# One core, gated long convolution plus a two-layer feed-forward block: row scales through DRAM, six-bank runs in the second transform stage, new stage shares

## Chip, cores and metric

The kernel runs on one core of one Trainium2 chip. The metric is the device time of one execution in microseconds (us). Before the change it is 1026.62 us, the median of 3 runs (1026.29 to 1029.05).

## What is computed

The inputs are x (called q in the first function), k and v of 2048 rows by 576 columns, all in float32; the feed-forward part has 4608 hidden columns.

```python
def _A_ref(q, k, v, shift_k, ssm_k, ssm_D):
    k_shift = sum over t < 4 of k_pad[:, t:t+S, :] * shift_k[:, 3-t]      # short causal filter
    kv = k_shift * v
    kv_f, kf_f = rfft(kv padded to 2S), rfft(ssm_k padded to 2S)          # long causal filter
    y = irfft(kv_f * kf_f)[:S] + kv * ssm_D
    return q * y
def _B_ref(x, w1, w2):
    return relu(x @ w1) @ w2

xn = layernorm(x)
return x + _A_ref(xn, k, v, shift_k, ssm_k, ssm_D) + _B_ref(xn, w1, w2)
```

(The sums and transforms of the first function are written short here.)

## The kernel before

**Two streams in one program.** The feed-forward part ("FFN") is the main program. The convolution ("conv") is a Python generator, `conv()`, whose steps are put between the FFN's instructions while the program is written down. So one order per engine holds both, and an engine that waits at the head of its order keeps everything behind it waiting.

**The FFN.** The 16 row tiles t of 128 rows form 4 blocks; two halves of two blocks are worked one after the other. For each half there are 18 groups of 256 hidden columns, so 36 groups ("quads", L630) g in all. In a quad the hidden sums of two blocks are made by products in a Strassen-like form: `product` (L575, six matmuls of 512 columns, high and low parts of operands and weights) and `rest` (L584, two matmuls) write two PSUM banks `psh`, that trade roles as x and y. VectorE and ScalarE add, negate and take the relu between products: u2 (L686), the negated copy L688 (`x = -y`, which must have read bank y before the next `rest` writes there), p5 (L693), and `hidden` (L589), which writes the high part hh on ScalarE and the low part ll on VectorE (L595). Between the products stand eight "units" (`mm2`, L726): 12 matmuls of 288 columns into one of two double banks `pso` (tags o0, o1), then an addition to the accumulator on VectorE (L752). A unit is opened (its bank pair taken) one unit ahead, L635. Weights come by GpSimd's queue (`load_w1`, `load_w2`), ScalarE and GpSimd split them into high and low parts (L514, L515). The first three groups are done plainly (`classical`, L598); from then on the operands are multiplied by each row's 1/std.

**Row scales before.** `inv_std` (L190) gives rstd, one value per row, with rows on partitions. The operands have rows along the free axis, so the scale must be spread over all partitions: eight VectorE instructions build diagonal matrices (`diagonal`, L315), two float32 matmuls with a matrix of ones sum them (`scales`, L323, L327), two ScalarE copies leave PSUM (L330), and `scaled` multiplies (L340).

**The conv's stages**, in order: (FB) rows of the second half are normalised and transposed on VectorE (`later_operands`, L403); (FS) 14 steps combine and split operands and store them (L461 to L476), and from n = 6 on every second step loads one of 16 blocks of the long filter (`load_filter`, L807, on GpSimd's queue); the other blocks follow with a pause KT_GAP each (L865); (FK) 32 filter copies and 11 groups of first-stage transforms, with matrices loaded by GpSimd's queue (`load_mat`, L817); (FX) the short filter ("taps", L937 to L949, eight VectorE instructions per tile t) and 9 groups of input transforms; (FM) the second stage: 18 chunks n, each with the filter's spectrum, the product with the input's spectrum, a join, and the way back; (FO) 16 tiles of inverse first-stage transforms, gate and addition.

**FM before.** A step takes PE for a "run" of matmuls in 64x64 tiles: `product_of(n)` fills two `psf` banks and, in a borrowed `pso` pair, the spectrum n + 1 (16 matmul records); VectorE multiplies (L1051, four instructions), ScalarE copies the spectrum out (L1024, two), SP's queue swaps halves by eight DMAs (L1029, L1056). `join(n)` (L1063) at the start of the next step adds what the L1056 transfers brought. After every second chunk a run of its own, `way_back` (L1065), takes two chunks back: two narrow banks and a borrowed pair.

**Order and pace.** `tick` (L1180) is called with each FFN piece's columns. It advances the conv's clock by `rate` times the columns and takes up to two steps of the generator while that clock is not negative; a step costs its W_ constant. A run that borrows a bank pair is put only after a product or a rest and only if a unit has closed since the last borrowing. A negative yield is a pause in FFN columns. The constants are L57 to L63, the rate is L1173, so a stage's share of the FFN's columns is its number of steps by its W_ over `CONV_TOTAL`.

```python
rate = CONV_TOTAL / (SHARE * FFN_TOTAL - PAUSES * PAUSE - 12 * KT_GAP)
```

Of the kernel before, what the change touches and what calls it, by code (L numbers as in the profile page):

```python
# [99 lines left out]
def h3_ffn_kernel(ctx: ExitStack, tc, x, k, v, shift_k, ssm_k, ssm_D, w1, w2, fwd, inv, mid, out):  # L100
# [29 lines left out]
    hl_n = dram.tile([HB, P, 512], F32, name="hl_n")  # L130

# [183 lines left out]
    def diagonal(pool, b):  # L315
        diag = pool.tile([P, 2, D], F32, tag="xn", name=f"diag{b}", bufs=4)
        diag = diag[:, 0, :BT * P].rearrange("p (i n) -> p i n", i=BT)
        for i in range(BT):
            nc.vector.tensor_scalar(diag[:, i, :], ident, rstd[:, b * BT + i:b * BT + i + 1],
                                    None, op0=OP.mult)  # L320
        return diag

    def scales(pool, b, diag):  # L323

        ps = fft_psum()
        with tc.issue_after(done["pe"].ins):
            done["pe"] = nc.tensor.matmul(ps, ones, diag.rearrange("p i n -> p (i n)"),  # L327
                                          start=True, stop=True)
        row[b] = pool.tile([P, 512], F32, tag=f"row{b}", name=f"row{b}")
        nc.scalar.activation(row[b], ps, AF.Copy)  # L330
# [72 lines left out]
    def later_operands(view, views, load_filter):  # L403
# [8 lines left out]
        for t0 in range(first, T, 4):  # L412
            for t in range(t0, t0 + 4):
                with here():
                    stats(t, rows[t - t % 2][:, t % 2, :])
                yield W_FB / 2
            with here():
                inv_std(t0, 4)
            yield W_FB / 2
# [169 lines left out]
    def hidden(g, b, f, ps):  # L589
# [3 lines left out]
        done["act"] = nc.scalar.activation(hh, ps, AF.Relu)  # L593
        with tc.issue_after(done["centred"].ins):
            nc.vector.scalar_tensor_tensor(ll, ps, 0.0, hh, op0=OP.max, op1=OP.subtract)  # L595
        hid[g, b, f] = (hh, ll)

# [32 lines left out]
    def quad(g, units):  # L630


        def unit(n):
            if n + 1 < len(units):
                open_unit(*units[n + 1], n + 1 in stage["seeded"] and more)  # L635
            mm2(*units[n])
            post(1)
# [9 lines left out]
        open_unit(*units[0])  # L647
# [41 lines left out]
        hidden(g, 0, 1, u2)  # L689
# [4 lines left out]
        hidden(g, 1, 1, p5)  # L694
# [11 lines left out]
        hidden(g, 1, 0, x)  # L706

# [5 lines left out]
    stage = {"seeded": ()}  # L713
    seeded = set()

# [10 lines left out]
    def mm2(g, b, i):  # L726
# [5 lines left out]
        cols = slice(i * P, (i + 1) * P)  # L732
        ps, slot["closed"] = open_ps.pop((g, t))
# [67 lines left out]
    def stages(view, views):  # L801
# [5 lines left out]
        def load_filter():  # L807
            if blocks:
                d, h = blocks.pop(0)
                src = ssm_k[h * NH + d:h * NH + d + KD, :].rearrange("d (p t) -> p d t", t=A2)  # L810
                with here():
                    nc.gpsimd.dma_start(kt[halves(h)[0], d:d + KD, :], src)  # L812
# [4 lines left out]
        def load_mat(key, t):  # L817
            nc.gpsimd.dma_start(mats.put(key), fwd[t])
# [49 lines left out]
        for t in range(2):  # L868
            load_mat(("k", t), t)
# [47 lines left out]
        for e, t2 in enumerate(order):  # L917
# [13 lines left out]
            if e % U and e // U + 2 < T:  # L931
                load_mat(("k", e // U + 2), e // U + 2)
# [109 lines left out]
        def product_of(n):  # L1042
# [4 lines left out]
            leave = second_spectrum(n + 1) if n + 1 in pairs_n else lambda: None  # L1047
# [9 lines left out]
            leave()  # L1057
            load(zx, n + 2, "x")
# [6 lines left out]
        def way_back(n):  # L1065


            narrow, wide = [fft_psum() for _ in range(2)], borrowed()
            for i, banks in enumerate((narrow, [wide[:, k, :] for k in range(2)])):
                turn(banks, [(1, parts[0][n + i])])  # L1070
            for k in range(2):
                with here():
                    nc.scalar.activation(backs[:, k, :], narrow[k], AF.Copy)
            nc.sync.dma_start(both(zy, n), backs[:, :2])
            with here():
                nc.scalar.activation(backs[:, 2:], wide, AF.Copy)
            nc.sync.dma_start(both(zy, n + 1), backs[:, 2:])
# [8 lines left out]
        for n in range(NCH // 2 + 1):  # L1086
            if n in pairs_n:
                yield "wide"
            if n:
                join(n - 1)  # L1090
            if n in pairs_n:
                product_of(n)
            yield W_FMK / 2 + W_FMX
            if n and n % 2 == 0:
                yield "wide"
                way_back(n - 2)
            if n:
                yield W_FMK / 2 + W_FMB
# [74 lines left out]
    rate = CONV_TOTAL / (SHARE * FFN_TOTAL - PAUSES * PAUSE - 12 * KT_GAP)  # L1173
# [40 lines left out]
    ones = const.tile([P, P], F32, name="ones")  # L1214
    nc.vector.memset(ones, 1.0)
# [11 lines left out]
    with tc.tile_pool(name="fa", bufs=1) as fa:  # L1227
# [19 lines left out]
        diag = {b: diagonal(fa, b) for b in (1, 0)}  # L1247

        def unit(g, b, i, upto):
            open_unit(g, b, i)  # L1250
# [33 lines left out]
    for b in range(2):  # L1284
        for i in range(BT):
            open_unit(QUADS - 1, b, i)
            mm2(QUADS - 1, b, i)
# [28 lines left out]
```

## Time and profile before

The profile is of one execution. Its own span is 1026.2 us; the three timed runs took 1029.05, 1026.29 and 1026.62 us, so the span and the time of such an execution lie within half a microsecond of each other.

| Engine | busy, us | share of the span |
|---|---|---|
| PE (matmul) | 1011.8 | 99% |
| PEld (weight load) | 845.9 | 82% |
| VectorE (DVE) | 709.2 | 69% |
| GpSimd (POOL) | 486.8 | 47% |
| ScalarE (ACT) | 429.7 | 42% |

The stages lie in the span about so: FB 124 to 173 us, FS 175 to 237, filter blocks to 245, FK 285 to 379, taps 394 to 657, FM 667 to 914, FO 929 to 1005. A timeline row gives start, length, engine, line, what is written from what, how many instructions are merged, and in brackets the idle time before it with what ended it. In a table by windows each engine has its busy time in that stretch and, in parentheses, its instructions; PEclk is the granted clock as a share of full speed.

### The profile page before, as it was taken

How to read it: one execution, taken by the hardware profiler on the slowest of the kernel's cores; microseconds unless marked ns; L12 is line 12 of the kernel's file. 1: busy time of each engine (PE TensorE's matmuls, PEld its weight loads, DVE VectorE, ACT ScalarE, POOL GpSimd, SP SyncE). 2: the span in 40 equal slices, each digit the busy share in tenths (PEclk: the TensorE clock that was granted, in tenths of full speed). 3: DMA queues.
4: the chain of work that ended last, by engine and by line, in shares of the span. 5: the costliest groups of instructions: out<-in, count | busy, mean ns of one | idle time of the engine just before them, and what ended most of it. 6: DMA issues, size and time to landing. Idle time of an engine off the chain costs nothing.

```text
span 1026.2 us, 17380 instructions
## 1 busy us (share of the span) xinstructions
PE 1011.8 (99%) x6506; PEld 845.9 (82%) x6506; DVE 709.2 (69%) x1075; ACT 429.7 (42%) x761; POOL 486.8 (47%) x532
## 2 busy tenths in 40 slices
PE   9999999999999999999999999989999999999997
PEld 5898999998988889888878889867767777788777
DVE  6787677776465567779787889456656676656765
ACT  7244334443344444444434444444535355332220
POOL 4335446659544557555545455414423344344450
PEclk9999999999999999999999999999999999999999
DMA  7114467558245565369943433677778887857784
GB/s 177 48 44 117 116 173 168 181 175 200 73 134 174 179 196 146 112 208 370 277 139 125 137 97 115 205 222 222 228 227 245 236 264 238 225 189 238 207 256 116
DMA packets 92249, 184.70 MB, mean 180 GB/s; under 512 B 32082, under 2 KB 44500, under 8 KB 91268
## 3 DMA queue, kind: packets, MB, share of 16 engines
q1 hardware_dynamic: 73588, 123.47, 39.8%
q0 software_dynamic: 18256, 59.22, 20.0%
q10 hardware_dynamic: 320, 0.88, 0.3%
q8 instruction: 51, 0.84, 0.3%
q14 instruction: 34, 0.28, 0.1%
HBM read 119.04 MB, written 45.61 MB: 160 GB/s over the span
## 4 chain that ended last, share of the span: by engine, by line
PE 87%; DVE 4%; POOL 2%; DMA 2%; issue 2%; ACT 1%; SPq 1%; DVEq 0%; POOLq 0%; ACTq 0%
PE pso L571 40%; PE psh L571 34%; PE psf L765 5%; PE psg L765 4%; PE psh_c L571 3%; DMA area<-area 1%; POOL area L812 1%; PE psw L1223 1%; DMA r<-in_w 1%; DVE area L944 1%; DVE area L1051 1%; DVE area L945 0%; SPq L1029 0%; DVE sums L527 0%; DVE x L295 0%
## 5 line engine op out<-in xcount | busy, mean ns | idle before, releaser
L571 PE MATMUL pso<-w,hh 128*128 128x288 f32 x2304 | 468.4, 297 | 0.0
L571 PEld LDWEIGHTS pso<-w,hh 128*128 128x128 f32 x2304 | 378.6, 188 | 34.8 <-issue 15.6
L571 PE MATMUL pso<-w,ll 128*128 128x288 f32 x1152 | 340.0, 295 | 0.0
L752 DVE TENSOR_TENSOR acc<-pso,acc 128x576 f32<-128x576 f32 x243 | 183.0, 754 | 157.4 <-PE pso L571 157.1
L571 PEld LDWEIGHTS pso<-w,ll 128*128 128x128 f32 x1152 | 216.8, 188 | 0.0
L515 POOL TENSOR_TENSOR wb<-sums,wb 128x512 fp32r<-128x512 f32 x33 | 51.2, 1552 | 236.1 <-ACT wb L514 208.5
L515 POOL TENSOR_TENSOR w<-r,w 128x576 fp32r<-128x576 f32 x72 | 107.8, 1505 | 106.9 <-ACT w L514 105.8
L571 PE MATMUL psh<-x,wa 128*128 128x512 f32 x396 | 102.9, 395 | 0.5 <-POOL wa L515 0.3
L571 PE MATMUL psh<-xs,wb 128*128 128x512 f32 x396 | 102.0, 393 | 0.0
L571 PE MATMUL psh<-hl,wr 128*128 128x512 f32 x264 | 85.9, 407 | 6.3 <-ACT psh L688 6.3
L571 PEld LDWEIGHTS psh<-x,wa 128*128 128x128 f32 x396 | 72.3, 188 | 16.1 <-POOL wa L515 0.8
L571 PEld LDWEIGHTS psh<-xs,wb 128*128 128x128 f32 x396 | 70.8, 188 | 11.4
L515 POOL TENSOR_TENSOR wa<-r,wa 128x512 fp32r<-128x512 f32 x36 | 53.7, 1490 | 52.8 <-ACT wa L514 52.8
L595 DVE SCALAR_TENSOR_TENSOR ll<-psh,hh 128x512 fp32r<-128x512 f32 x66 | 45.2, 685 | 40.9 <-ACT hh L593 40.7
L688 ACT ACTIVATE psh<-psh 128x512 f32<-128x512 f32 x33 | 19.2, 582 | 128.2 <-DVE u L686 128.2
L571 PEld LDWEIGHTS psh<-hl,wr 128*128 128x128 f32 x264 | 46.0, 188 | 27.1 <-issue 13.2
L765 PE MATMUL psf<-area 64*64 64x512 f32 (+10 forms) x592 | 61.1, 473 | 0.0
L593 ACT ACTIVATE hh<-psh 128x512 fp32r<-128x512 f32 x66 | 39.4, 597 | 49.7 <-PE psh L571 49.0
L765 PE MATMUL psg<-area 64*64 64x512 f32 (+10 forms) x568 | 55.3, 453 | 0.0
L593 ACT ACTIVATE hh<-p 128x512 fp32r<-128x512 f32 x33 | 20.9, 632 | 79.1 <-DVE p L693 43.2
L1024 ACT ACTIVATE area<-psg 128x1024 f32<-128x1024 f32 x34 | 33.2, 1025 | 48.7 <-PE psg L765 48.1
L1051 DVE TENSOR_TENSOR area<-psf,area 128x512 f32<-128x512 f32 x72 | 44.7, 681 | 9.4 <-DMA area<-area 6.7
(140 smaller groups left out, 1525.1 us busy)
## 6 DMA issues: line engine op xcount, KB each, us to landing
r<-in_w POOLq DMA_DIRECT2D x70, 288.0 KB, 3.4
area<-area SPq DMA_DIRECT2D x144, 128.0 KB, 3.8
r<-in_w POOLq DMA_DIRECT2D x35, 512.0 KB, 5.1
zk<-area SPq DMA_DIRECT2D x64, 144.0 KB, 2.3
area<-zk SPq DMA_DIRECT2D x18, 512.0 KB, 4.5
area<-zx SPq DMA_DIRECT2D x18, 512.0 KB, 3.9
zy<-area SPq DMA_DIRECT2D x18, 512.0 KB, 4.8
area<-zy SPq DMA_DIRECT2D x32, 288.0 KB, 5.4
```

Of the source, the lines that this page charges most:

```text
L515: nc.gpsimd.tensor_tensor(w[:, 1, :n], src, w[:, 0, :n], OP.subtract)
L571: last = nc.tensor.matmul(ps, a, m, start=start and n == 0, stop=n == len(seq) - 1, skip_group_check=True)
L593: done["act"] = nc.scalar.activation(hh, ps, AF.Relu)
L595: nc.vector.scalar_tensor_tensor(ll, ps, 0.0, hh, op0=OP.max, op1=OP.subtract)
L688: nc.scalar.activation(x, y, AF.Copy, scale=-1.0)
L752: done["acc"] = nc.vector.tensor_tensor(two(acc[t]), ps[:, :, :NH], two(acc[t]), OP.add)
L765: done["pe"] = nc.tensor.matmul(ps, a, m, start=start, stop=stop, skip_group_check=True)
L812: nc.gpsimd.dma_start(kt[halves(h)[0], d:d + KD, :], src)
L944: nc.vector.tensor_tensor(e, win[t - n], sk[:, n, :], OP.mult)
L1024: nc.scalar.activation(dst, src, AF.Copy)
L1051: nc.vector.tensor_tensor(filt[c][:, k, :], banks[k], filt[c][:, k, :], OP.mult)
L1223: last = nc.tensor.matmul(idle[0], warm[:, :P], warm, start=True, stop=True)
```

## The change

Five edits, the core of the diff below (other constants and hunks of one line are left out or told here):

1. `diagonal`, `scales` and the ones matrix go. `spread_scales` copies rstd, transposes it in 32x32 blocks on VectorE, stores it in DRAM by four small transfers (SP's and ScalarE's queues, two each) and reads it back by two transfers that repeat each block's 512 values on all 128 partitions, row 1 first. It stands where `diagonal` stood.
2. In FM a step's run now holds the way back of chunk n - 2, the product n and the spectrum n + 1: six banks, 24 records. To have both `pso` pairs for it, no unit is opened ahead in FM (`stage["lazy"]`). The order on the engines after the run is: copy of the way back, four multiplications, copies of the spectrum.
3. Costs W_, KT_GAP and the rate are new; every FS step from n = 6 on loads a filter block, so eight are left for the loop with pauses instead of twelve.
4. Filter blocks and the matrices of FK are issued by SP's queue instead of GpSimd's. From n = 6 on the third staging place of FS is the place of operand "11" instead of one that filter blocks take.
5. In a quad two low parts come later: ll of (0, 1) behind the addition p5, ll of (1, 1) behind ll of (1, 0). In FB the normalisation of 8 row tiles moves from VectorE to ScalarE, with a shift computed by one small VectorE instruction per four tiles.

```diff
-KT_GAP = 3200
+KT_GAP = 6000
-W_FB, W_FS, W_FK, W_FX, W_FMK, W_FMX, W_FMB, W_FO = 2.8, 4.1, 2.5, 1.75, 4.0, 3.6, 2.9, 3.9
+W_FB, W_FS, W_FK, W_FX, W_FMK, W_FMX, W_FMB, W_FO = 2.6, 3.0, 1.9, 2.2, 4.0, 3.5, 2.9, 3.9
...
-    def borrowed():
+    def borrowed(first=False):
         slot["lent"] = slot["units"]
-        return ps_o.tile([P, 2, 512], F32, tag=f"o{slot['closed']}", name="psg")
+        n = 1 - slot["open"] if first else slot["closed"]
+        return ps_o.tile([P, 2, 512], F32, tag=f"o{n}", name="psg")
...
+    def spread_scales(pool):
+        sq, turned = (pool.tile([P, 32], F32, tag=f"sq{n}", name=f"sq{n}") for n in range(2))
+        nc.vector.tensor_copy(sq, rstd[:, :2 * BT].unsqueeze(1).to_broadcast([P, 4, 2 * BT]))
+        nc.vector.transpose(turned, sq)
+        for q in range(P // 32):
+            queue = nc.scalar if q % 2 else nc.sync
+            queue.dma_start(scale_n[:, 32 * q:32 * q + 32], turned[32 * q:32 * q + 2 * BT])
+        for b in (1, 0):
+            row[b] = pool.tile([P, 512], F32, tag=f"row{b}", name=f"row{b}")
+            src = scale_n[b * BT:(b + 1) * BT].rearrange("(o i) p -> o (i p)", o=1)
+            nc.sync.dma_start(row[b], src.to_broadcast([P, 512]))
...
-                    normalized(pair[:, t % 2, :], pair[:, t % 2, :], t)
+                    nc.scalar.activation(pair[:, t % 2, :], pair[:, t % 2, :], AF.Identity,
+                                         scale=rstd[:, t:t + 1], bias=shift[:, t - t0:t - t0 + 1])
...
+                if n == HB * 3:
+                    stages_o.views = (*stages_o.views[:2], yf["11"])
...
-                if n >= 6 and n % 2:
+                if n >= 6:
                     load_filter()
...
-        hidden(g, 0, 1, u2)
+        low = hidden(g, 0, 1, u2, True)
...
         nc.vector.tensor_tensor(p5, y, p5, OP.add)
-        hidden(g, 1, 1, p5)
+        low()
+        low = hidden(g, 1, 1, p5, True)
...
         hidden(g, 1, 0, x)
+        with tc.issue_after(done["ll"].ins):
+            low()
...
-                    nc.gpsimd.dma_start(kt[halves(h)[0], d:d + KD, :], src)
+                    nc.sync.dma_start(kt[halves(h)[0], d:d + KD, :], src)
...
+        stage["lazy"] = True
+        while open_ps:
+            yield W_FX
+        for n in pairs_n:
+            yield "wide"
             if n:
                 join(n - 1)
+            back = back_wide(n - 2, n + 1 in pairs_n) if n > 1 else None
+            made = product_of(n)
+            leave = second_spectrum(n + 1) if n + 1 in pairs_n else None
+            if back:
+                back()
+            multiplied(n, *made)
+            if leave:
+                leave()
+            load(zx, n + 2, "x")
+            yield W_FMK + W_FMX + W_FMB
+        yield "wide"
+        join(NCH // 2 - 1)
+        backs_left = back_narrow(NCH // 2 - 2), back_wide(NCH // 2 - 1, False)
...
-    rate = CONV_TOTAL / (SHARE * FFN_TOTAL - PAUSES * PAUSE - 12 * KT_GAP)
+    rate = CONV_TOTAL / (SHARE * FFN_TOTAL - PAUSES * PAUSE - 8 * KT_GAP)
...
-        diag = {b: diagonal(fa, b) for b in (1, 0)}
+        spread_scales(fa)
...
-                if g == 1:
-                    scales(fa, 1 - f, diag[1 - f])
```

More of the change, by code (lines that the diff above doesn't have):

```diff
@@ L313, in h3_ffn_kernel @@
     row = {}
[L315 to L330, printed above, removed]
+    def spread_scales(pool):
[9 more added lines that the diff above has]
+            nc.sync.dma_start(row[b], src.to_broadcast([P, 512]))
     def scaled(o, b):
@@ L633, in unit @@
         def unit(n):
-            if n + 1 < len(units):
-                open_unit(*units[n + 1], n + 1 in stage["seeded"] and more)
+            if n + 1 < len(units) and not stage["lazy"]:
+                open_early(*units[n + 1], n + 1 in stage["seeded"] and more)
             mm2(*units[n])
@@ L646, in quad @@
         y = bank(g, 1, "2")
-        open_unit(*units[0])
+        if not stage["lazy"]:
+            open_early(*units[0])
         product(x, wa[g], 0, "00", start=True, g=g, place=False)
@@ L711, in h3_ffn_kernel, with open_early @@
     open_ps = {}
-    stage = {"seeded": ()}
+    stage = {"seeded": (), "lazy": False}
     seeded = set()
+    def open_early(g, b, i, seed=False):
+        if (g, token(g, b, i)) not in open_ps:
+            open_unit(g, b, i, seed)
     def open_unit(g, b, i, seed=False):
@@ L1063, in join, with way_back, leave, back_wide @@
                 nc.vector.scalar_tensor_tensor(to, other, sign, to, op0=OP.mult, op1=OP.add)
[L1065 to L1077, printed above, removed]
+        def way_back(n, banks, copied):
+            turn(banks, [(1, parts[0][n])])
+            to = backs[:, 2 * (n % 2):2 * (n % 2) + 2]
+            def leave():
+                for dst, src in copied(to):
+                    with here():
+                        nc.scalar.activation(dst, src, AF.Copy)
+                nc.sync.dma_start(both(zy, n), to)
+            return leave
+        def back_wide(n, first):
+            wide = borrowed(first)
+            return way_back(n, [wide[:, k, :] for k in range(2)], lambda to: [(to, wide)])
+        def back_narrow(n):
+            banks = [fft_psum() for _ in range(2)]
+            return way_back(n, banks, lambda to: [(to[:, k, :], banks[k]) for k in range(2)])
         for n in range(2):
```

48 lines of the change are left out of this document (23 added, 25 removed).

## The prediction

> **What bounds the kernel now.** First the page: its span and the engines' busy time.
>
> ```profile
> span 1026.2 us, 17380 instructions
> ...
> PE 1011.8 (99%) x6506; PEld 845.9 (82%) x6506; DVE 709.2 (69%) x1075; ACT 429.7 (42%) x761; POOL 486.8 (47%) x532
> ```
>
> PE has work in 99% of the span, so only two things can shorten it: PE instructions that go, and stretches in which PE waits or runs below its rate. The table of waits, for PE alone, says what it waits for:
>
> ```profile
> PE psh L571 <- ACT psh L688: 6.3, 3, 2.7
> ...
> PE psh L571 <- POOL wa L515: 0.3, 1, 0.3
> ```
>
> Three waits make almost all of it. VectorE at 69% matters only where it delays such a wait; DMA and ScalarE likewise. I took these places one by one in the timeline, then looked for PE work that the change drops. The sum is made against the span of 1026.2 us; the median of the runs, 1026.62, is 0.4 above it, and I subtract from the median.
>
> **Row scales (edit 1).** The timeline around the two matmuls with the matrix of ones:
>
> ```profile
> 29.76 0.20 DVE L190 RECIPROCAL rstd<-q 128x8 f32<-128x8 f32 x1
> ...
> 32.38 0.29 PE L571 MATMUL pso<-w,ll 128*128 128x288 f32 x1
> ...
> 32.97 1.12 PE L327 MATMUL psf<-diag,ones 128*128 128x512 f32 x2 [0.29 <-DVE diag L319]
> 33.53 3.33 PE L571 MATMUL psh_c<-x,wa 128*128 128x512 f32 x12
> ...
> 40.20 0.29 PE L571 MATMUL pso<-w,ll 128*128 128x288 f32 x1
> 40.34 1.02 PE L327 MATMUL psf<-diag,ones 128*128 128x512 f32 x2
> ...
> 40.79 1.95 PE L571 MATMUL psh_c<-x,wb 128*128 128x512 f32 x6
> 41.27 1.89 DVE L340 TENSOR_TENSOR xf<-xf,row 128x512 f32<-128x512 f32 x3
> ...
> 42.58 1.54 PE L571 MATMUL psh_c<-x,wd 128*128 128x512 f32 x6
> ...
> 45.30 0.69 DVE L595 SCALAR_TENSOR_TENSOR ll<-psh_c,hh 128x512 fp32r<-128x512 f32 x1 [2.14 <-ACT hh L593]
> ...
> 50.64 0.29 PE L571 MATMUL pso<-w,ll 128*128 128x288 f32 x1
> 50.78 2.92 PE L571 MATMUL psh_c<-x,wa 128*128 128x512 f32 x12
> ```
>
> Where nothing lies between, the next product starts 0.14 us after the last unit matmul (50.64 to 50.78) and twelve take 2.92. At the first scale the product starts 33.53 - 32.38 - 0.14 = 1.01 later and its twelve take 0.41 more: 1.42. At the second it is 40.79 - 40.20 - 0.14 = 0.45, and six take 1.95 against 1.54: 0.86. Both go: **-2.3 us** of PE.
>
> In their place come two small VectorE instructions and a trip through DRAM, which no row shows. The nearest rows are a store of 144 KB and a load that repeats one row on 128 partitions:
>
> ```profile
> zk<-area SPq DMA_DIRECT2D x64, 144.0 KB, 2.3
> ...
> area<-in_shift_k POOLq DMA_DIRECT2D x4, 288.0 KB, 5.9
> ```
>
> rstd is there at 29.96; VectorE then has an ll until 30.85 and the two new instructions, some 0.2 each as the small one at 29.76 is. From 31.25: two issues per queue (about 1 us), landing 2.3, an issue, landing 5.9: row 1 at about 41. It is wanted at 41.27 less the 1.42 that PE has gained, 39.85; VectorE would wait about 1 us there. Behind it in VectorE's order stand three L340 (1.89 us) and the ll at 45.30, which waits 2.14 us for other things, so up to about 2 us of lateness cost nothing. Bounds: 0 if it lands by 42; if either transfer takes twice its row, some 3 us of PE. I take 0, as the trip is 8.2 of a free 10 to 12 us.
>
> **Six-bank runs (edit 2).** What a run costs beside its matmuls comes from the first run, of 8 records, and one of 16:
>
> ```profile
> 667.15 1.09 PE L765 MATMUL psf<-area 64*64 64x512 f32 x8
> 668.17 0.54 PE L571 MATMUL pso<-w,hh 128*128 128x288 f32 x2
> ...
> 910.97 0.63 PE L571 MATMUL psh<-hl,wr 128*128 128x512 f32 x2
> 911.53 1.09 PE L765 MATMUL psf<-area 64*64 64x512 f32 x8
> ...
> 913.40 0.53 PE L571 MATMUL pso<-w,hh 128*128 128x288 f32 x2
> ```
>
> From run start to the next FFN matmul: 1.02 for 8, 1.87 for 16; so 8 records cost 0.85 and a run 0.17 on top. Going in costs too: the two matmuls before take 0.56 instead of 2 x 0.243 (a twelfth of 2.92): 0.07. A run is worth 0.24 us. Before, the stage has 1 + 18 + 9 = 28 runs (the first spectrum, the products, the ways back); after, 1 + 18 + 1 = 20. Eight fewer: **-1.9 us**.
>
> The opposite bill: with no unit opened ahead, a unit right behind a run writes the pair that the way back has just left. Its copy, and what that engine did before such copies:
>
> ```profile
> L1024 ACT ACTIVATE area<-psg 128x1024 f32<-128x1024 f32 x34 | 33.2, 1025 | 48.7 <-PE psg L765 48.1 <-DMA area<-area 0.7
> ```
>
> The way back is first in the run: done 0.85 in, copied 1.03 later, 1.9 to 2.1; the run ends at 0.17 + 3 x 0.85 = 2.72. ScalarE may be 0.6 late without cost. It stood idle for 48.1 us before 17 such copies, 2.8 each, so mostly it is free in time. Bounds: 0, or about 0.5 at each of 16 steps, 8 us, if two weight splits stood before every copy. I take **+1.0**.
>
> **The waits (edits 2 and 3).** The places where PE waits or is slow:
>
> ```profile
> 519.49 0.68 DVE L686 TENSOR_TENSOR u<-psh,u 128x512 f32<-128x512 f32 x1
> ...
> 520.85 1.12 PE L571 MATMUL psh<-hl,wr 128*128 128x512 f32 x2 [1.95 <-ACT psh L688]
> ...
> 679.37 1.80 PE L765 MATMUL psf<-area 64*64 64x512 f32 x8
> ...
> 688.60 0.68 DVE L686 TENSOR_TENSOR u<-psh,u 128x512 f32<-128x512 f32 x1
> ...
> 689.95 0.74 PE L571 MATMUL psh<-hl,wr 128*128 128x512 f32 x2 [2.69 <-ACT psh L688]
> ...
> 755.02 0.73 PE L571 MATMUL psh<-hl,wr 128*128 128x512 f32 x2 [1.67 <-ACT psh L688]
> ```
>
> All three long ones are one chain: u2 on VectorE is late behind conv work, L688 waits for it, `rest` for L688. At 689.95 and 755.02 the conv work is the four multiplications, held by swaps not yet landed. Chunk 0 costs the conv's clock only W_FMK/2 + W_FMX = 5.6, so chunk 1 follows it 5 us later, which also makes the run at 679.37 take 0.71 more than the 1.09 above. After, every step costs 10.4 and holds one run, so I let these go: -2.69, -1.67, -0.71. At 520.85 it is taps. There the FX share grows from 146 x 1.75 at a rate of 708.7 per 1,460,631 columns to 146 x 2.2 at 733.4 per 1,451,031: 526,600 to 635,500 columns, x1.207. VectorE's load, whole and of the conv alone, by windows:
>
> ```profile
> 174.00:237.00 63.00, 63.00 (x385) 57.65 (x384) 46.22 (x69) 28.99 (x55) 36.22 (x34) 1.00 0.59 183
> 500.00:660.00 160.00, 157.98 (x1035) 136.85 (x1034) 130.32 (x172) 72.84 (x129) 78.27 (x79) 0.99 0.47 143
> ...
> 174.00:237.00 63.00, 0.00 (x0) 0.00 (x0) 18.59 (x22) 8.76 (x14) 6.69 (x6) 1.00 0.59 183
> 500.00:660.00 160.00, 11.74 (x168) 5.27 (x168) 72.62 (x76) 12.03 (x18) 4.45 (x8) 0.99 0.47 143
> ```
>
> In the taps 130.32/160 = 81% becomes (57.7 + 72.62/1.207)/160 = 74%: -1.95. FS pays: 14 x 4.1 + 8 x 1.4 = 68.6 becomes 14 x 3.0 + 8 x 1.3 = 52.4, in columns x0.733, so VectorE there goes from 73% to 27.6/63 + 18.59/(0.733 x 63) = 84% for some 46 us. The taps at 81% lost 1.95 + 1.7 (below) in 160 us; 46/160 of that is **+1.0** (0 to one whole, 3.7). And since which unit a burst meets is chance, I put in one new wait of the mean size of the old three, **+2.1**.
>
> After the wait at 518.9 PE ran slowly for a while:
>
> ```profile
> 521.00:523.00 2.00, 2.00 (x8) 1.81 (x9) 2.00 (x4) 0.33 (x1) 0.00 (x0) 0.50 0.48 137
> 523.00:525.00 2.00, 2.00 (x10) 1.92 (x10) 1.30 (x3) 0.40 (x1) 0.00 (x0) 0.65 0.00 0
> ```
>
> Granted 0.50 and 0.65: 1.0 + 0.7 = 1.7 us lost, and gone with the wait: -1.7. The Trainium skill ("TensorE: Matmul & The Clock Gate", Why this matters for your kernels) says that idle gaps of more than some 3 us halve the clock; by that a gap of 1.95 would not, and the sum would be 1.7 smaller. The trace disagrees: here 1.95 did, while the 2.69 at 687 did not.
>
> **Queues (edit 4).** GpSimd's filter blocks stand before a wait:
>
> ```profile
> 234.99 6.89 POOL L812 DMA_DIRECT2D area<-in_ssm_k x6
> ```
>
> Six issues hold GpSimd 6.89 us; weight splits queue behind them, and the 0.3 wait on wa at 254 is the last of it. **-0.3.** On SP the blocks stand between the stores of FS, the matrices between those of FK; behind a waiting one are the next stores, and who waits for those is the next copy into the staging view. A block's place is empty when its turn comes (that is what the moved staging place does), so I cost it at 0; bounds 0 to 3.7, one held-up VectorE as in the taps.
>
> **Edit 5** moves work that PE does not wait for (no ll is in its table), with ScalarE at 42% taking the normalisations: 0; if that cover fails, one wait of 2.
>
> **Sum.** -2.3 - 1.9 - 2.69 - 1.67 - 0.71 - 1.95 - 1.7 - 0.3 = -13.2; +1.0 + 1.0 + 2.1 = +4.1; -9.1. 1026.6 - 9.1 = **1017.5 us**.
>
> **Rivals.**
>
> *The waits only move* (0.22). The structural part stays, -2.3 - 1.9 - 0.3 = -4.5, and as many u2 waits arise as go; with FS and copies 0 to +2, 1022.1 to 1024.1, middle 1023.1. For it: a burst of four multiplications is as long as before. Against: two of three waits come from transfers not landed in short steps.
>
> *The pair is not free in time* (0.07): slower. If ScalarE's copy of the way back starts only after the whole run, each of 16 steps with a unit next pays 1.03 + 0.1 and the spectrum copies shift behind it: 16 x 1.13 = 18 us, so 1026.6 - 13.2 + 18 = 1031.5. It decides from 16.3/16 = 1.0 us per step. Against it, banks are read while their run goes on:
>
> ```profile
> 738.13 1.09 PE L765 MATMUL psf<-area 64*64 64x512 f32 x8
> ...
> 739.39 2.47 DVE L1051 TENSOR_TENSOR area<-psf,area 128x512 f32<-128x512 f32 x4
> ...
> 740.00 0.53 PE L571 MATMUL pso<-w,hh 128*128 128x288 f32 x2
> ```
>
> VectorE starts 1.26 into a run of 1.87.
>
> *The scales come late* (0.08), so edit 1 does not do what it says: a trip of 16 us instead of 8 stops VectorE at 39.85, accumulators behind it, about 3 us of PE: 1020.5.
>
> **How the numbers follow.** Forecast 0.63, the others 0.22, 0.07, 0.08. Low end: all -13.2 and nothing new, 1013.4; of the 14.4 us without a matmul (1026.2 - 1011.8) the three waits hold 6.3, so some small ones may go too: 1012.5. High end: the waits that only move, with the upper bounds of FS or SP (3.7) in part, 1025. 0.3% is 3.1 us, about what a measurement of this kernel can tell from no change: faster is below 1023.5. That holds the forecast, the late scales and half of the moving waits: 0.63 + 0.08 + 0.11 = 0.82; same 0.11; slower 0.07.
>
> **What would show it.** Right: no L327, products 0.14 after units near 32 and 39 us, L340 not waiting for a transfer; 20 runs in FM, of 2.7 us with 24 records; PE's waits on L688 below 3 us in all, no window at half clock; no wait on wa near 254. Wrong: unit matmuls waiting for ScalarE's copies right behind runs (the slow rival), new waits on L688 in FS or FM (the moving one), VectorE standing before L340.

## The result and the profile after

The changed kernel takes 1019.18 us, median of 5 runs (1018.47 to 1021.45); the kernel before takes 1027.03 on the same chip (1026.29 to 1029.05, 5 runs). The ratio is 0.9929, 95% interval 0.9914 to 0.9943: by the medians 7.9 us faster, where the prediction was 9.1.

The run records hold time and span side by side: a run takes about 1.75 us more than its span (1019.7 and 1021.45 here). So the profiled execution of before, span 1026.2, took about 1028.0. That is 1 us above its median and not 0.4 below, as the prediction had it; that of after is the slowest of its five.

The page of after, its span and engines, and what the DMA engines moved:

```profile
span 1019.7 us, 17381 instructions
...
PE 1004.9 (99%) x6502; PEld 844.4 (83%) x6502; DVE 697.7 (68%) x1059; ACT 436.8 (43%) x765; POOL 460.5 (45%) x500
...
DMA packets 129720, 185.22 MB, mean 182 GB/s; under 512 B 69042, under 2 KB 83508, under 8 KB 128740
```

and the last of these on the page of before:

```profile
DMA packets 92249, 184.70 MB, mean 180 GB/s; under 512 B 32082, under 2 KB 44500, under 8 KB 91268
```

PE is busy 6.9 us less. The bytes differ by half a megabyte, which is what the two row loads bring (2 times 256 KB), but there are 37,471 more packets, 36,960 of them under 512 B. The table of PE's waits after:

```profile
PE psh L575 <- DVE p L704: 2.2, 1, 2.2
PE psg L785 <- issue: 1.5, 1, 1.5
...
PE psh L575 <- ACT psh L661: 1.0, 1, 1.0
...
PE psh L575 <- ACT psh L699: 0.8, 1, 0.8
```

The wait of 6.3 us on the negated copy (now L699) is down to 0.8. A new one on p5 (L704) stands at the top, and one of 1.5 inside a run. The 1.0 on L661, an earlier negated copy of the quad, is new too; it stands in FS, at 210.8 us.

**The scales** in the timeline of after, at the two places where the matrix of ones stood, and the group of the new loads:

```profile
32.39 0.29 PE L575 MATMUL pso<-w,ll 128*128 128x288 f32 x1
...
32.52 2.93 PE L575 MATMUL psh_c<-x,wa 128*128 128x512 f32 x12
...
38.80 0.29 PE L575 MATMUL pso<-w,ll 128*128 128x288 f32 x1
38.93 1.55 PE L575 MATMUL psh_c<-x,wb 128*128 128x512 f32 x6
39.13 0.82 DVE L768 SCALAR_TENSOR_TENSOR acc<-pso,rstd,acc 128x576 f32<-128x576 f32 x1 [0.78 <-PE pso L575]
39.87 1.89 DVE L338 TENSOR_TENSOR xf<-xf,row 128x512 f32<-128x512 f32 x3
```

```profile
L328 SPq DMA_DIRECT2D row<-scale_n x2: 347/390/432, 34.0 to 34.4; - x2
...
DMA to landing us min/median/max: 4.6/4.7/4.9
```

The products follow 0.13 us behind the units and take 2.93 and 1.55, their undisturbed lengths. The rows land 4.7 us after issues at 34.0 and 34.4, so by about 39, and the multiplications follow the accumulation without a wait.

**FM.** One step of after: the end of the units, the run of 24 records, its readers, and the unit that follows at once:

```profile
743.94 0.63 PE L575 MATMUL psh<-hl,wr 128*128 128x512 f32 x2
...
744.50 1.09 PE L785 MATMUL psg<-area 64*64 64x512 f32 x8
...
745.70 1.03 ACT L1094 ACTIVATE area<-psg 128x1024 f32<-128x1024 f32 x1 [2.83 <-issue]
...
746.60 2.48 DVE L1074 TENSOR_TENSOR area<-psf,area 128x512 f32<-128x512 f32 x4
...
747.23 0.53 PE L575 MATMUL pso<-w,hh 128*128 128x288 f32 x2
```

The run lasts 747.23 - 744.50 = 2.73 us (forecast 2.72). The copy of the way back starts 1.20 into it and ends at 746.73, half a microsecond before the unit wants the pair. No PE wait in the profile is put down to these copies. There are 20 runs, 15 of them with 24 records. Only the last waits, for the last join:

```profile
903.14 1.09 PE L785 MATMUL psf<-area 64*64 64x512 f32 x8
...
904.34 1.28 DVE L1084 SCALAR_TENSOR_TENSOR area<-area,sign 128x1024 f32<-128x1024 f32 x1 [0.80 <-DMA area<-area]
...
905.72 1.09 PE L785 MATMUL psg<-area 64*64 64x512 f32 x8 [1.50 <-issue]
```

The join starts when its transfer has landed and ends at 905.62; the second half of the run begins 0.1 later.

**FS** lost time. The timeline of after around the new wait on p5:

```profile
193.76 4.82 SPq L476 DMA_DIRECT2D ops_s<-area  x1
...
201.60 1.73 SPq L476 DMA_DIRECT2D ops_s<-area  x1
201.63 0.63 ACT L473 ACTIVATE area<-area 128x512 fp32r<-128x512 f32 x1 [2.66 <-DMA ops_s<-area]
202.30 0.69 DVE L474 TENSOR_TENSOR area<-area 128x512 fp32r<-128x512 f32 x1 [2.60 <-ACT area L473]
...
204.18 0.68 DVE L704 TENSOR_TENSOR p<-psh,p 128x512 f32<-128x512 f32 x1
...
204.91 1.65 PE L575 MATMUL psh<-x,wa 128*128 128x512 f32 x6 [2.23 <-DVE p L704]
```

Read from below: PE waits for p5; p5 stands on VectorE behind L474, with an accumulation and one more conv instruction between them; VectorE had stood idle 2.60 before L474, for ScalarE's copy L473; ScalarE had waited 2.66 before that for a store's transfer, since its staging place was still being read. The stores' issues and landings changed with what stands before them on SP. First before, then after, from the tables of DMA issues between 160 and 240 us:

```profile
ops_s<-area SPq DMA_DIRECT2D x8, 512.0 KB, 3.1
area<-in_ssm_k POOLq DMA_DIRECT2D x13, 288.0 KB, 6.9
```

```profile
area<-in_ssm_k SPq DMA_DIRECT2D x16, 288.0 KB, 6.2
ops_s<-area SPq DMA_DIRECT2D x8, 512.0 KB, 7.8
```

and the issue itself, minimum, median and maximum in ns, by groups of before and of after:

```profile
L812 POOL DMA_DIRECT2D area<-in_ssm_k x16: 1154/1162/1183, 169.2 to 244.9; - x16
```

```profile
L832 SPq DMA_DIRECT2D area<-in_ssm_k x16: 613/1616/4447, 161.1 to 233.1; - x16
L476 SPq DMA_DIRECT2D ops_s<-area x8: 512/1122/4817, 183.5 to 230.4; - x8
```

A block costs GpSimd a steady 1.16 us, but up to 4.4 on SP, and the store behind it up to 4.8; a store lands 7.8 us after its issue instead of 3.1.

To see where time went, I took from each profile the moment at which u2 (L686 before, L697 after) of five quads starts, and the difference to the profiled execution of before. The marks lie at 101, 246, 465, 652 and 937 us of before; a column is what its stretch gained (-) or lost (+), in us. All kernels of the study are in it; the sections below use it.

```
kernel          start  FB,FS  FK+taps  taps   FM     sum
after           -2.3   +3.8   +1.9     -3.3   -6.9   -6.7
after_again     -1.9   +2.9   -0.4     -3.4   -7.7  -10.4
a_pool          -1.9   +2.6   +0.5     -3.0   -6.8   -8.6
a_slow_fs       -2.1   +3.2   +8.6     -4.3   -6.4   -1.0
a_mix           -1.6   +1.2   -0.4     -3.5   -6.2  -10.4
a_mix_end       -2.0    0.0   +0.2     -3.3   -7.3  -12.4
a_low_now       -2.1   +2.3   +0.5     -2.3   -7.7   -9.3
a_old_shares    -2.3    0.0   +0.6     -3.6   -0.1   -5.5
b_sp            -0.4    0.0   -0.6     -2.4   +1.9   -1.5
b_scales        -1.3    0.0   +2.2     -3.5   +0.1   -2.5
b_six           -0.1    0.0   +1.9     -3.3   -1.3   -2.7
b_shares        +0.4   +0.2   +1.0     -3.0   +5.5   +4.1
b_six_shares    +0.6   +0.3   +1.5     -3.0   -7.6   -8.2
```

(a_ kernels start from the changed kernel, b_ kernels from the kernel before. One profile each: after and after_again are the same kernel and differ by 0.1 to 0.9 us in four columns and by 2.3 in the third, so differences of such sizes mean little.)

### The profile page after: what moved, and what is told of

The parts are those of the page before. It is cut to its first block, busy times and chain, and to the rows that moved or that the text cites. A ratio compares the mean times of both kernels' runs of the same rounds, so it can differ in the third digit from the quotient of the medians.

```text
span 1019.7 us, 17381 instructions
## 1 busy us (share of the span) xinstructions
PE 1004.9 (99%) x6502; PEld 844.4 (83%) x6502; DVE 697.7 (68%) x1059; ACT 436.8 (43%) x765; POOL 460.5 (45%) x500
## 2 busy tenths in 40 slices
DMA packets 129720, 185.22 MB, mean 182 GB/s; under 512 B 69042, under 2 KB 83508, under 8 KB 128740
## 4 chain that ended last, share of the span: by engine, by line
PE 90%; DMA 4%; DVE 3%; issue 1%; ACT 1%; POOL 1%; SPq 0%; DVEq 0%; POOLq 0%; ACTq 0%
PE pso L575 42%; PE psh L575 34%; PE psg L785 5%; PE psf L785 4%; PE psh_c L575 3%; DMA ops_s<-area 1%; DMA r<-in_w 1%; DMA zk<-area 1%; PE psw L1260 1%; DVE ll L602 1%; DVE sums L531 0%; DVE x L297 0%; PE psx L235 0%; SPq L910 0%; POOL wd L519 0%
## 5 line engine op out<-in xcount | busy, mean ns | idle before, releaser
L772 DVE TENSOR_TENSOR acc<-pso,acc 128x576 f32<-128x576 f32 x240 | 180.4, 754 | 123.9 <-PE pso L575 123.3
L519 POOL TENSOR_TENSOR wb<-sums,wb 128x512 fp32r<-128x512 f32 x33 | 47.6, 1441 | 291.8 <-ACT wb L518 266.2
L519 POOL TENSOR_TENSOR wa<-r,wa 128x512 fp32r<-128x512 f32 x36 | 56.5, 1570 | 54.0 <-ACT wa L518 53.9
L699 ACT ACTIVATE psh<-psh 128x512 f32<-128x512 f32 x33 | 19.2, 582 | 117.4 <-DVE u L697 117.4
L785 PE MATMUL psg<-area 64*64 64x512 f32 (+10 forms) x632 | 64.2, 472 | 1.5 <-issue 1.5
L697 DVE TENSOR_TENSOR u<-psh,u 128x512 f32<-128x512 f32 x33 | 22.8, 691 | 45.3 <-PE psh L575 45.2
L785 PE MATMUL psf<-area 64*64 64x512 f32 (+10 forms) x528 | 51.1, 451 | 0.7 <-DVE area L941 0.7
L575 PE MATMUL psh<-xs,wc 128*128 128x512 f32 x198 | 51.2, 393 | 0.0
```

What stands on the lines that cost most here:

```text
L519: nc.gpsimd.tensor_tensor(w[:, 1, :n], src, w[:, 0, :n], OP.subtract)
L575: last = nc.tensor.matmul(ps, a, m, start=start and n == 0, stop=n == len(seq) - 1, skip_group_check=True)
L697: nc.vector.tensor_tensor(u2, x, u2, OP.add)
L699: nc.scalar.activation(x, y, AF.Copy, scale=-1.0)
L772: done["acc"] = nc.vector.tensor_tensor(two(acc[t]), ps[:, :, :NH], two(acc[t]), OP.add)
L785: done["pe"] = nc.tensor.matmul(ps, a, m, start=start, stop=stop, skip_group_check=True)
```

## The experiments

The theory after the result: edits 1 to 3 pay as the sum had them, and the loss in FS comes from edit 4, blocks in front of stores on SP. Rivals: the loss in FS comes from its denser steps (edit 3); the gain in FM and the taps comes from places alone, by chance. Four of the first eight kernels put edits 1 to 4 into the kernel before one at a time (of edit 4 the filter blocks alone); the last four follow from what these showed.

**after_again**: the changed kernel once more, no edit, to see what of its profile repeats.

> The changed kernel once more, on the chip of the three others: the yardstick for the two variants of it. Both theories expect 0.993 of before (1027 to 1019 us), and again some 3.5 us of PE waiting between 200 and 212 us.

1018.75 us (ratio 0.9919, 0.9905 to 0.9933; before 1027.20 us, measured beside this kernel and the next three). The waits at 204 and 210 us come again (1.35 and 1.02), and a shorter one in the last run: the loss in FS belongs to the kernel.

**a_pool**: the blocks back on GpSimd's queue.

```diff
-                    nc.sync.dma_start(kt[halves(h)[0], d:d + KD, :], src)
+                    nc.gpsimd.dma_start(kt[halves(h)[0], d:d + KD, :], src)
```

> The changed kernel, with the 16 filter blocks issued by GpSimd's queue again and nothing else undone. Theory of the queue: SP's long issues of filter blocks (up to 4.4 us each) make the operand stores late, so the two PE waits at 203 to 211 us (2.4 + 1.2) go, and a wait on wa of some 0.5 may come back: 1016 us, 0.3% under the changed kernel. Theory of the pace: the waits stay, because the stage has too few columns for VectorE's work: 1019 us.

1019.90 us (0.9927, 0.9915 to 0.9939), no better. The waits at 203 to 211 are gone, which fits the theory that SP's queue made them; but the time that this theory expected (1016) did not come, and another wait stands 20 us later, in the timeline of a_pool:

```profile
214.31 6.91 POOL L832 DMA_DIRECT2D area<-in_ssm_k  x6 [4.90 <-DMA ops_s<-area]
...
217.69 3.10 DVE L531 TENSOR_TENSOR sums<-r 128x256 f32<-128x256 f32 x2
...
220.71 3.81 DVE L531 TENSOR_TENSOR sums<-sums,r 128x256 f32<-128x256 f32 x2
...
224.44 0.68 DVE L697 TENSOR_TENSOR u<-psh,u 128x512 f32<-128x512 f32 x1
...
225.78 0.73 PE L575 MATMUL psh<-hl,wr 128*128 128x512 f32 x2 [2.39 <-ACT psh L699]
```

GpSimd waited 4.90 us for a store that still read a staging place and then issued six blocks in a row. Beside that burst and the weight splits behind it, VectorE's additions of two SBUF operands took 3.10 and 3.81 for two, where two mostly take 0.75 to 0.9; u2 came late, and PE waited 2.39. That the issues themselves slow the additions is not shown: in the same profile five other additions beside block issues, at 170 and 195 us, took 0.41 to 0.42 each, and the last two of the four here overlap GpSimd's weight splits, which stand behind the burst.

**a_slow_fs**: FS at its old step cost, to test its density.

```diff
-W_FB, W_FS, W_FK, ... = 2.6, 3.0, 1.9, ...
+W_FB, W_FS, W_FK, ... = 2.6, 4.1, 1.9, ...
```

> The changed kernel with W_FS at 4.1 instead of 3.0 and nothing else undone: the stage of the operands gets its old time, all others about 2% less. Theory of the pace: the two waits at 203 to 211 us go, 1016 us. Theory of the queue: filter blocks still sit in SP's queue before the stores; with more time between steps a part of the 3.6 us goes, but issues above 3 us and waits of ScalarE for the stores stay: 1017.5 us.

1026.70 us (0.9999, 0.998 to 1.0019): all of the gain is gone, which neither theory had expected (1016 and 1017.5). A wait in FS stays (2.09 us, ended at 210.26), so the pace of the steps is not its cause. FK, pushed later, loses 8.6 us; its longest wait, on copies held by stores of zk, is followed by half the clock (in a table by windows the granted clock is the third number from the end; it stays so to 360 us):

```profile
356.86 0.85 PE L575 MATMUL pso<-w,hh 128*128 128x288 f32 x2 [3.25 <-DVE area L869]
```

```profile
356.80:358.00 1.20, 1.14 (x5) 1.14 (x6) 1.20 (x4) 0.50 (x1) 0.79 (x3) 0.51 1.05 240
```

**b_sp**: the blocks on SP's queue in the kernel before, where they come at every second step.

```diff
-                    nc.gpsimd.dma_start(kt[halves(h)[0], d:d + KD, :], src)
+                    nc.sync.dma_start(kt[halves(h)[0], d:d + KD, :], src)
```

> The kernel before, with only the 16 filter blocks moved to SP's queue. Theory of the queue: issues of some 1.6 us and more on SP and late operand stores here too, though the steps are slower and only every second one loads a block; the wait on wa at 254 us (0.5) goes, a wait of 0 to 2 us comes: 1027 to 1028.5. Theory of the pace: only the wait on wa goes: 1026.5.

1026.70 us (0.9991, 0.9979 to 1.0002). The wait on wa at 254 goes, and FS loses nothing: SP's queue alone does no harm when a block stands before every second store only.

**b_scales**: edit 1 alone in the kernel before (the new `spread_scales` and its place; `diagonal`, `scales` and the matrix of ones go).

> The kernel before with only the row scales by transfers. Prediction: both scale matmuls go, 2.3 us, VectorE does not wait before L340: 0.9978 of before. Rival (the scales come late): a gap on VectorE before its first multiplication and less than 1 us gained.

1026.05 us (0.999, 0.9971 to 1.0008; before 1026.94 us, measured beside this kernel and the next three): 0.9 us, where the prediction gives the edit 2.3. The interval, 3.0 us faster to 0.8 slower, holds both 2.3 and nothing, so the time alone doesn't decide. In its profile the start gains 1.3 us; the long waits of FM are there (2.74 and 1.51), and one of 1.26 is new, at 461.9 us.

**b_six**: edit 2 alone in the kernel before (the step of FM with three chunks, the lazy pairs).

> The kernel before with only the second transform stage of the change: six-bank runs, no unit opened ahead there, old costs W_. If the gain of that stage is its own (fewer runs 1.9, even steps that leave no long wait 5), it is 6 to 7 us: 0.9935 of before. If the even pace came from the new shares, it is 1.9 us, 0.998, and the waits behind u2 in the stage stay.

1023.26 us (0.9965, 0.9952 to 0.9978). FM's two long waits on the negated copy (2.69 and 1.67) are gone under the old shares too, so the stage's own form takes them away. But its last run waits for the last join, more than twice as long as in after:

```profile
906.01 1.28 DVE L1072 SCALAR_TENSOR_TENSOR area<-area,sign 128x1024 f32<-128x1024 f32 x1 [2.23 <-DMA area<-area]
...
907.40 1.99 PE L773 MATMUL psg<-area 64*64 64x512 f32 x8 [3.73 <-issue]
```

```profile
905.60:909.00 3.40, 1.60 (x8) 0.34 (x8) 1.89 (x2) 0.00 (x0) 0.00 (x0) 0.50 0.41 159
```

3.73 us of waiting, then half the clock, to 912.4 us: the 8 matmuls take 1.99 where they take 1.09. That is most of what FM gains here less than in after.

b_six also tells something of the taps. Up to 655 us its instructions on PE, VectorE, ScalarE and GpSimd are those of before, in the same order; only FM differs. At the place where before waits 1.95 us and then runs at half the clock, it has

```profile
520.91 0.74 PE L572 MATMUL psh<-hl,wr 128*128 128x512 f32 x2 [0.42 <-ACT psh L690]
```

and no half clock behind it. So two executions of the same instructions differ there.

**b_shares**: edit 3 alone in the kernel before, with the staging place.

```diff
-KT_GAP = 3200
+KT_GAP = 6000
...
-W_FB, W_FS, W_FK, W_FX, W_FMK, W_FMX, W_FMB, W_FO = 2.8, 4.1, 2.5, 1.75, 4.0, 3.6, 2.9, 3.9
+W_FB, W_FS, W_FK, W_FX, W_FMK, W_FMX, W_FMB, W_FO = 2.6, 3.0, 1.9, 2.2, 4.0, 3.5, 2.9, 3.9
...
-                if n >= 6 and n % 2:
+                if n >= 6:
```

> The kernel before with only the new costs W_, KT_GAP, a filter block at every step from n = 6 and the staging place that goes with it; blocks still by GpSimd. By the profile after: the wait in the taps and the half clock go (3.6 us), the operand and filter stages pay about as much (3 to 4 us), the second transform stage keeps its waits: 0.999 to 1.001 of before. If the shares were worth their part of the gain, 0.996.

1033.21 us (1.0058, 1.0039 to 1.0077): slower by 6, which neither side of the expectation had. Its profile is of the fastest of its six runs, 1029.78, so it shows a part of the loss only: up to 652 us it does as the others, it loses 5.5 in FM, still in its old form there, and 2.3 come back behind the last mark. Its two longest waits in the timeline:

```profile
706.65 1.67 PE L573 MATMUL psh<-xs,wc 128*128 128x512 f32 x6 [2.43 <-DVE ll L597]
...
884.66 0.74 PE L573 MATMUL psh<-hl,wr 128*128 128x512 f32 x2 [3.29 <-ACT psh L690]
```

FS, with a block by GpSimd at every step, loses 0.2 here.

**a_mix**: the changed kernel with its blocks shared out: the eight within FS by GpSimd, one per step, the eight in the pauses by SP.

```diff
-        def load_filter():
+        def load_filter(queue=nc.sync):
...
-                    nc.sync.dma_start(kt[halves(h)[0], d:d + KD, :], src)
+                    queue.dma_start(kt[halves(h)[0], d:d + KD, :], src)
...
-                    load_filter()
+                    load_filter(nc.gpsimd)
```

> The changed kernel, with the eight filter blocks inside the operand steps issued by GpSimd and the eight in the pauses by SP. Seen so far: all on SP, stores of operands land late and PE waits 2.7 to 3.6 us at 203 to 211; all on GpSimd, six issues in a row from 214 us on, VectorE's sums run at 1.5 to 2 us instead of 0.4 beside them, PE waits 2.6 at 223. If these are two causes, one per queue, both waits go: 1016 us, 0.3% under the changed kernel. If both come from the amount that is moved by DMA in the stage, a wait of 2 to 3 us stays somewhere between 200 and 226: 1019.

1016.89 us (0.9905, 0.9887 to 0.9923): below both kernels, by the ratios 1.4 to 2.5 us below the changed one (0.9919 and 0.9929 in its two measurements, with intervals that overlap this one). FS loses 1.2 instead of 2.9 to 3.8, with neither SP's held-up stores nor a burst on GpSimd; a wait of 0.79 at 208.7 is left there. The last run is now PE's longest wait, 1.9.

**a_mix_end**: in that kernel the last run is cut in two, so that the way back that needs no join goes first.

```diff
         yield "wide"
+        back_narrow(NCH // 2 - 2)()
+        yield W_FMB
+        yield "wide"
         join(NCH // 2 - 1)
-        backs_left = back_narrow(NCH // 2 - 2), back_wide(NCH // 2 - 1, False)
-        for leave in backs_left:
-            leave()
+        back_wide(NCH // 2 - 1, False)()
         yield W_FMB
```

> The kernel with the blocks shared out (eight by GpSimd in the loop, eight by SP in the pauses; 1016.89 us), and in it the last run of FM cut in two: the narrow way back of chunk 16 goes first, as it needs no join, and the join and the way back of chunk 17 follow a step later. If PE's last wait in FM (1.5 to 1.9 us in these kernels) is the last join's arrival alone: the wait goes, one more run costs 0.24, so 1.3 to 1.7 less, 1015.2 to 1015.6. Rival: the join comes late for reasons of VectorE's order and the wait moves with it: 1016.9 to 1017.2, with a wait on L785 of over 1 us still there.

1016.87 us (0.9896, 0.988 to 0.9912; before 1028.11 us, measured beside this kernel and the next three). The wait in the profile falls from 1.9 to 0.8, not to nothing, and a run is added; in the time it can't be told from a_mix. The rival's value came, though the wait fell below the 1 us that it had named.

**b_six_shares**: edits 2 and 3 together in the kernel before, nothing else.

> The kernel before with the new FM stage and the new shares (costs, pause, a block at every FS step, the staging place), without the scales, SP's queue and edit 5. Theory 1, the shares' loss of 6 us lies in the old FM stage, whose two runs per two chunks they set badly: with the new stage the loss is gone and the gain of the new shares in the taps shows, 1020 to 1022. Theory 2, the parts add: -3.6 + 6.2 = 2.6 above before, 1029.5. Theory 3, places alone: anything between, with waits of over 1 us at places that neither kernel has.

1019.04 us (0.9919, 0.9904 to 0.9934): the first theory's side, 1 below its range, and 10 below the sum of the two parts. These two edits together, without 1, 4 and 5, give the whole time of after. In its profile FM gains 7.6 and the last run waits 0.7.

**a_old_shares**: the changed kernel with the old costs, pause and every second step.

> The kernel after with the old costs, pause and every second FS step with a block. Theory 1, the shares trade FS and FK (4.8 us lost after) against the taps and FM (3.65 gained in the taps): 1018 to 1020 with the wait of about 2 us in the taps back, and the one at 203 to 211 us gone. Theory 2, the six-bank stage needs the new shares: waits in FM come back, 1022 and more.

1020.07 us (0.9933, 0.9916 to 0.995), at the upper end of the first theory, and for other reasons than it had. FS loses nothing, with the blocks on SP, at every second step. The wait in the taps is not back (the longest there is 0.39 us). FM gives back its gain at one place, the last run, as in b_six; of the second theory this much is true:

```profile
904.28 1.98 PE L785 MATMUL psg<-area 64*64 64x512 f32 x8 [3.37 <-issue]
```

```profile
906.00:908.00 2.00, 2.00 (x11) 1.81 (x8) 0.00 (x0) 1.02 (x1) 0.00 (x0) 0.50 0.01 4
```

**a_low_now**: the low parts of edit 5 written where they stood.

```diff
-        low = hidden(g, 0, 1, u2, True)
+        hidden(g, 0, 1, u2)
...
-        low()
-        low = hidden(g, 1, 1, p5, True)
+        hidden(g, 1, 1, p5)
...
-        with tc.issue_after(done["ll"].ins):
-            low()
```

> The kernel after with the two low parts of a quad written where they stood before (edit 5's first half undone). Theory 1, as the prediction had it, PE waits for no low part and the edit is worth 0: 1018.5 to 1019.5. Theory 2, the late low parts free VectorE for u2 and p5, whose waits are what decides: 0.7 us later for them in some quads, so waits on L688 and on the product behind p5 come back, 1020 to 1023.

1019.19 us (0.9919, 0.9899 to 0.9938): the first theory; the later low parts are worth nothing here.

## Why the prediction was right, and where its steps were wrong

The time came inside the range and on the forecast's side, 1.2 us from the forecast in the difference. That it came so close is in part luck: FM gained 6.9 to 7.7 us where the sum had 6.0 (1.9 + 5.07 - 1.0), FS lost 2.9 to 3.8 where it had 1.0, and the 3.65 of the taps came for another reason than the one given. By its own steps:

- **Scales, -2.3: right.** The start gains 1.6 to 2.3 in the changed kernel and its variants, though 1.3 in b_scales; the trip through DRAM ended by about 39, two microseconds earlier than worked out, and nothing waits for it. The rival of late scales is refuted.
- **Eight runs fewer, -1.9, and FM's waits, -5.07: right.** 20 runs, 2.73 us for 24 records, no long wait on the negated copy in FM. b_six shows that the stage's form alone does it.
- **The pair not ready, +1.0: not there.** The copy is done before the run ends, so the slow rival (the pair not free in time) is refuted too. FM's gain of 6.9 in after holds one new wait, 1.5 in the last run, where the sum put 2.1 for one at an unknown place.
- **The taps, -1.95 and -1.7: failed as reasoning.** "There the FX share grows" was the reason, by VectorE's load of 81% falling to 74%. The load did fall, to 114.17 of 160 us, 71%, and the wait and the half clock did go in after. But the stretch is shorter in every other kernel of the study too, -2.3 to -4.3 in the fourth column, b_sp, b_scales, b_six and a_old_shares with the old shares among them: at the same place b_sp waits 1.05, b_scales 0.69 and b_six 0.42, none with half a clock behind it. As b_six has the same instructions up to there, the wait's length was that of one execution; a long wait in one profile was counted as the kernel's.
- **FS, +1.0 for denser steps, and edit 4 at 0: both sizes were wrong.** Steps as dense with GpSimd's blocks cost 0.2 to 0.3 in the kernel before (b_shares, b_six_shares); blocks on SP at every second step cost 0 (b_sp, a_old_shares); SP's blocks at every step cost 2.3 to 3.8 (after, after_again, a_low_now, and a_slow_fs with slower steps). The step that failed is "A block's place is empty when its turn comes (that is what the moved staging place does), so I cost it at 0": not the place was missing, but SP's time. The bound of 3.7 given for it is about what came. SP is not the only way to this loss: in the changed kernel GpSimd's blocks cost 2.6 as well (a_pool), by another wait, and why the same blocks cost b_shares so little stays open. The rival "the waits only move" holds for this stage at most, and the new waits there are on p5 and L661, not on the copy behind u2.
- **POOL's wait, -0.3, and edit 5, 0: right.** The wait on wa is gone in b_sp and in after. The low parts are worth nothing in a_low_now; the normalisations on ScalarE were not undone alone, but b_six_shares, without any of edit 5, takes the same time as after.
- **What the sum could not see** is that edits 2 and 3 don't add. Alone they give 0.9965 and 1.0058, together 0.9919. Two things are shown in the profiles: under the old shares the last run meets a join that has not landed (3.4 and 3.7 us and half the clock, in both kernels of that kind), and under the new shares the old FM stage meets new waits. Why the old stage does so at these places, and why the old shares bring the last run to its join too early, was not taken apart and stays open.

So edits 2 and 3 are enough for the gain; by the table the scales' 2 us and the loss on SP in FS about cancel, and a_mix, which mends most of that loss, takes some 2 us less. That edit 3 is needed is shown only where edits 1, 4 and 5 are absent: in the changed kernel the old shares cost about 1 us, and the intervals overlap (0.9916 to 0.995 in a_old_shares, 0.9905 to 0.9933 in after_again). Edit 2 is in every kernel that gained more than 0.2%; the changed kernel without it was not run.

Part of the gain is the clock: the mean granted clock of 23 runs of before is 0.9974 (0.995 to 0.999), that of ten of after 0.9989, which by the span is 1.5 us, an estimate. The size is that of the term of 1.7, but the old shares or the old stage alone do not bring it: the mean is 0.9967 in b_six, 0.9970 in b_shares and 0.9992 in b_six_shares. Where those stretches lay in runs without a profile can't be seen.

## What to carry to other kernels

A long wait in one profile of a kernel with two interleaved streams may be that execution's place and not the kernel's: take the terms from work that always goes (instructions, runs) and from chains that the change cuts, and check a wait in a second profile before it is counted. FM's waits of 2.69 and 1.67 came again in b_sp and b_scales and went with the stage; the one in the taps came again at about half its length or less. When a queue's issues are moved, count what stands behind each issue on the new queue and how often: here one small-piece load before every second store cost nothing, one before every store 2 to 4 us, and in one profile six in a row on the old queue were followed by a wait of 2.4. Test parts in pairs: here two that gave -3.6 and +6 gave -8 together.

## What the runs showed of the hardware

- The same 288 KB block becomes 2304 packets under 512 B on SP's queue that it does not become on GpSimd's (after against a_pool: 69042 - 32178 = 36864 for 16 blocks, so 128 B each). The Trainium skill ("DMA: Bandwidth & Descriptors", Issuing engine by pattern) gives simple loads to SP as the generally faster path. Here the landing is about as long (6.2 and 6.9 us), the issue is longer and uneven (0.6 to 4.4 us against 1.16), and stores behind it land in 7.8 instead of 3.1.
- VectorE's additions of two SBUF operands (the weight sums) have a median of 0.42 us with GpSimd idle. In the 14 profiles, 164 of them start while a weight split of GpSimd runs; 114 of these take over 0.7 us, and the median of the 164 is 1.40. Beside GpSimd's DMA issues alone there are 206, with a median of 0.41, and only two take over 0.7: the first two of a_pool's burst. The Trainium skill ("SBUF — State Buffer", SBUF: two separate sides) says that the two engines lock a shared pair of ports by whole instructions, for VectorE's operations with two SBUF inputs where GpSimd's operation reads SBUF; the traces agree for the splits. What slowed the two beside DMA issues stays open.
- After a wait of PE the clock is halved or not, and the length of the wait gives no clear bound. These are the waits and what followed in b_sp and b_scales, at the same place in the program:

```profile
686.77 1.16 PE L571 MATMUL psh<-hl,wr 128*128 128x512 f32 x2 [2.69 <-ACT psh L688]
```

```profile
686.90:689.00 2.10, 2.10 (x8) 1.91 (x9) 1.72 (x3) 0.35 (x1) 0.00 (x0) 0.50 1.04 252
```

```profile
687.60 0.73 PE L568 MATMUL psh<-hl,wr 128*128 128x512 f32 x2 [2.74 <-ACT psh L685]
```

```profile
687.60:689.60 2.00, 2.00 (x13) 1.91 (x14) 1.48 (x3) 0.48 (x1) 0.00 (x0) 1.00 1.08 301
```

  Behind 2.69 us the granted clock of b_sp is 0.50, behind 2.74 that of b_scales is 1.00; after 1.95 (before) it was halved, and after 3.29 (b_shares, 884.7 to 890) it was 1.00. How long it stays halved differs too: 3.4 us in before (521.0 to 524.4), 6.8 in b_six (905.6 to 912.4).

  By the rule of the Trainium skill that the prediction names ("TensorE: Matmul & The Clock Gate", Why this matters for your kernels), the 2.69 of b_sp and the 1.95 of before would not have halved it, and the 3.29 of b_shares would.
